# Scores of the global queries moved into the row-tiled run of the local scores, in two PSUM banks, and the last output tile in three pieces

## The chip, the cores and the metric

The kernel runs on one NeuronCore of a Trainium2 chip. The metric is the time on the device in microseconds (us). The profile of one execution covers a slightly shorter span (315.8 us where the time is 317.6), and all times inside an execution are counted from its start. Every run quoted here was fast: one core, granted TensorE clock 0.993 to 1.00.

TensorE does the matmuls and writes to PSUM, of which this kernel uses eight banks of 512 fp32 columns on 128 partitions. ScalarE (ACT) and VectorE (DVE) read the banks; POOL (GpSimd) casts inputs. The first matmul of a new tile waits until the last reader of the tile that had its bank before has ended; in the trace of the changed kernel it then starts some 53 ns later.

## The reference, cut to what matters

```python
# batch 8, heads 8, 512 local and 32 global positions, head size 64; window 32
s_g  = scale * q_g @ concat(k_g, k_l).T            # 32 global queries see all 544 keys
out_g = softmax(s_g) @ concat(v_g, v_l)
s_ll = where(|i - j| <= 32, scale * q_l @ k_l.T, -1e9)
s_lg = scale * q_l @ k_g.T                         # local queries see window and global keys
out_l = softmax(concat(s_lg, s_ll)) @ concat(v_g, v_l)
x = concat(out_g, out_l)  -> (4352, 512)           # tokens x (heads * head size)
h = x @ w_in                                        # 512 -> 2048
out = (h * clip(h + 3, 0, 6) / 6) @ w_out           # 2048 -> 512
```

## The kernel before: the parts that matter

The unit of the attention part is a pair of heads, `p` (32 pairs, 4 per batch `b`). The second matrix product pair (called MoE in the code) is cut into units that are dealt out between the steps of attention by `M(n)`: 16 units `u1` per batch (four matmuls of 512 columns into a bank psH, then a relu on ScalarE and a multiplication `gt` on VectorE that frees the bank), then 16 units `u2` (four matmuls into a bank po, copied out after four units). The loop over the last 24 pairs:

```python
psp = tile_pool(name="psp", bufs=7, space=PSUM)     # seven rotating banks
psg = tile_pool(name="psg", bufs=1, space=PSUM)     # one for the global output
...
    M(n[0])
    ...
    if p + 1 < NPAIR:
        emit_S2(p + 1)        # local scores: row-tiled, four banks psS
    M(n[1])
    if p + 1 < NPAIR:
        emit_SG(p + 1)        # global scores: full height, one bank psSG
    ...
    M(n[2])
    emit_AV(p)                # probabilities times values, two banks pav
    emit_PG(p)
    M(n[3])
```
```python
def emit_S2(p):
    pss = [ps_tile(f"psS{i}") for i in range(4)]
    for ch in range(2):
        for w in (*range(1, NT), 0):
            ...
            for e in range(2):                      # head e lies on 64 of the 128 rows
                r = slice(e * D, (e + 1) * D)
                nc.tensor.matmul(out=pss[2 * ch + e][:, w * P:(w + 1) * P],
                                 lhsT=kT[r, c0:c0 + P], rhs=qT[r, w * P:(w + 1) * P])
    ...                                             # four exponentials, four masks

def emit_SG(p):
    ps = ps_tile("psSG")
    qz = qgz[:, m, b].rearrange("p e s -> p (e s)") # 2 x 32 columns, half of them zeros by rows
    for u in range(NT + 1):                         # five matmuls, 128 rows, 64 columns
        c0 = u * KW if u < NT else D
        nc.tensor.matmul(out=ps[:, u * 2 * Sg:(u + 1) * 2 * Sg], lhsT=kT[:, c0:c0 + P], rhs=qz)
    nc.scalar.activation(out=Eg[:, 0:NT]..., in_=ps[:, 0:NT * 2 * Sg], func=EXP, ...)
    nc.scalar.activation(out=Eg[r, NT]..., in_=ps[r, NT * 2 * Sg:(NT + 1) * 2 * Sg], func=EXP, ...)
```

A row-tiled matmul here uses 64 of the array's 128 rows, and the two heads run side by side: in the trace their matmuls start in twos, 3 to 4 ns apart.

The softmax here doesn't subtract the row's maximum and nothing guards it: scores larger than these inputs give would overflow.

## Time and profile before

| | before |
|---|---|
| time, median | 317.6 us |
| TensorE busy | 96% |
| VectorE, ScalarE, POOL busy | 68%, 63%, 48% |
| pair period, in the stretch from 172 to 250 us | 8.34 to 8.45 us |

TensorE never waits in that stretch. "Busy" alone would not tell that: it needs the timeline, where the starts of successive TensorE rows leave no gap. The prediction shows the rows. Three lines belong beside them, the shapes of the two global-score exponentials and of the matmul, from the groups by shape (columns: operation, shapes, count | busy us, mean ns | idle before):

```profile
L358 ACT ACTIVATE Eg<-psSG 128x256 f16<-128x256 f32 x32 | 13.0, 406 | 1.2 <-PE psSG L357 1.1
L361 ACT ACTIVATE Eg<-psSG 32x64 f16<-32x64 f32 x32 | 6.9, 215 | 0.8
L357 PE MATMUL psSG<-qgz,kT 128*128 128x64 f16 x160 | 9.2, 193 | 0.8 <-DVE qgz L213 0.8
```

The mean of a matmul (193 ns) is its length from start to modelled end, not its share of the stream: the five follow one another every 29 ns.

### The profile page before, as it was taken

How to read it: one execution, taken by the hardware profiler on the slowest of the kernel's cores; microseconds unless marked ns; L12 is line 12 of the kernel's file. 1: busy time of each engine (PE TensorE's matmuls, PEld its weight loads, DVE VectorE, ACT ScalarE, POOL GpSimd, SP SyncE). 2: the span in 40 equal slices, each digit the busy share in tenths (PEclk: the TensorE clock that was granted, in tenths of full speed). 3: DMA queues.
4: the chain of work that ended last, by engine and by line, in shares of the span. 5: the costliest groups of instructions: out<-in, count | busy, mean ns of one | idle time of the engine just before them, and what ended most of it. 6: DMA issues, size and time to landing. Idle time of an engine off the chain costs nothing.

```text
span 315.8 us, 7343 instructions
## 1 busy us (share of the span) xinstructions
PE 304.3 (96%) x2688; PEld 161.9 (51%) x2688; DVE 213.9 (68%) x484; ACT 200.1 (63%) x417; POOL 152.6 (48%) x273
## 2 busy tenths in 40 slices
PE   6898899999999999999999999999999999999995
PEld 4554555545555555555555555555555544448444
DVE  5678688898765799569945996468943962479101
ACT  6657877887444985479844993589556941579000
POOL 3878987599866475764574558542511000000000
PEclk9999999999999999999999999999999999999999
DMA  7999999999999999999997999896642002100131
GB/s 207 243 295 333 302 300 317 213 185 211 217 201 238 180 183 191 180 229 193 181 154 152 215 187 205 177 232 106 114 103 86 17 19 83 66 2 1 37 98 66
DMA packets 140260, 53.05 MB, mean 168 GB/s; under 512 B 127552, under 2 KB 131904, under 8 KB 140224
## 3 DMA queue, kind: packets, MB, share of 16 engines
q1 hardware_dynamic: 138048, 52.32, 78.3%
q0 software_dynamic: 2176, 0.26, 2.0%
q8 instruction: 21, 0.34, 0.5%
q14 instruction: 15, 0.12, 0.2%
HBM read 35.13 MB, written 8.91 MB: 139 GB/s over the span
## 4 chain that ended last, share of the span: by engine, by line
PE 81%; DVE 8%; ACT 6%; issue 2%; DMA 2%; SPq 0%; POOL 0%
PE po L488 34%; PE psH L472 32%; PE psS L297 3%; DVE gt L479 3%; PE pav L383 2%; PE pav L386 2%; ACT t L477 2%; DVE xn L391 2%; DMA stg<-in_q_l_dram 2%; DVE E L304 2%; PE psSG L357 1%; PE psS L326 1%; ACT E L335 1%; PE po L500 1%; ACT E L301 1%
## 5 line engine op out<-in xcount | busy, mean ns | idle before, releaser
L488 PE MATMUL po<-wout,gt 128*128 128x512 f16 x528 | 122.6, 379 | 0.0
L472 PE MATMUL psH<-xt,win 128*128 128x512 f16 x512 | 119.6, 379 | 1.4 <-POOL win L174 1.0
L479 DVE SCALAR_TENSOR_TENSOR gt<-t,psH 128x512 f16<-128x512 f32 (+1 forms) x144 | 90.1, 652 | 20.9 <-ACT t L477 19.8
L477 ACT ACTIVATE t<-psH,half_col 128x512 f32<-128x512 f32 (+1 forms) x144 | 91.8, 670 | 18.0 <-PE psH L472 16.8
L472 PEld LDWEIGHTS <-win 128*128 128x128 f16 x576 | 53.1, 98 | 52.8 <-POOL win L174 1.8
L488 PEld LDWEIGHTS <-gt 128*128 128x128 f16 x528 | 48.4, 98 | 52.2
L304 DVE TENSOR_TENSOR E<-E,mk 128x512 f16<-128x512 f16 x96 | 51.3, 569 | 30.4 <-ACT E L301 29.0
L301 ACT ACTIVATE E<-psS 128x512 f16<-128x512 f32 x96 | 49.9, 605 | 13.5 <-PE psS L297 13.4
L492 ACT COPY ot<-po 128x512 f32<-128x512 f32 x16 | 9.4, 586 | 58.6 <-PE po L488 53.1
L140 POOL CAST kn<-stg 128x512 f16<-128x512 f32 x31 | 19.8, 640 | 34.7 <-DMA stg<-in_k_l_dram 33.1
L391 DVE TENSOR_TENSOR xn<-pav,rc 128x256 f16<-128x256 f32 x64 | 26.1, 422 | 1.3
L409 POOL TENSOR_TENSOR s<-Eg 128x128 f32<-128x128 f16 x24 | 10.4, 434 | 33.8 <-ACT Eg L358 32.6
L492 DVE COPY ot<-po 128x512 f32<-128x512 f32 x17 | 11.7, 690 | 21.2 <-PE po L488 21.1
L140 POOL CAST qn<-stg 128x512 f16<-128x512 f32 x31 | 20.3, 656 | 11.3 <-DMA stg<-in_q_l_dram 11.3
L140 POOL CAST vt<-stg 128x512 f16<-128x512 f32 x32 | 21.1, 658 | 9.7 <-DMA stg<-in_v_l_dram 9.4
L144 POOL COPY vb<-vt 64x512 f16<-64x512 f16 x32 | 20.2, 631 | 2.1
L383 PE MATMUL pav<-vt,E 128*128 128x65 f16 x256 | 20.1, 194 | 0.0
L386 PE MATMUL pav<-vb,E 128*128 128x65 f16 x256 | 19.9, 195 | 0.0
L335 ACT ACTIVATE E<-psS 128x512 f16<-128x512 f32 x32 | 16.9, 600 | 4.8 <-PE psS L326 4.8
L383 PEld LDWEIGHTS <-E 128*128 128x128 f16 x256 | 17.9, 99 | 3.4
L386 PEld LDWEIGHTS <-E 128*128 128x128 f16 x256 | 16.8, 97 | 3.2
L297 PEld LDWEIGHTS <-kT 64*128 64x128 f16 x384 | 10.9, 94 | 10.1 <-issue 8.1
(93 smaller groups left out, 274.1 us busy)
## 6 DMA issues: line engine op xcount, KB each, us to landing
stg<-in_k_l_dram SPq DMA_DIRECT2D x32, 256.0 KB, 3.5
stg<-in_q_l_dram SPq DMA_DIRECT2D x32, 256.0 KB, 4.1
stg<-in_v_l_dram SPq DMA_DIRECT2D x32, 256.0 KB, 4.9
out_dram<-ot SPq DMA_DIRECT2D x23, 256.0 KB, 3.6
stg<-in_moe_w_in_dram SPq DMA_DIRECT2D x16, 256.0 KB, 6.0
stg<-in_moe_w_out_dram SPq DMA_DIRECT2D x16, 256.0 KB, 5.1
out_dram<-ot SPq DMA_DIRECT2D x8, 192.0 KB, 3.9
out_dram<-ot SPq DMA_DIRECT2D x16, 64.0 KB, 2.4
```

Of the source, the lines that this page charges most:

```text
L140: eng.tensor_copy(out=o, in_=s[c + "f"])
L297: nc.tensor.matmul(out=pss[2 * ch + e][:, w * P:(w + 1) * P], lhsT=kT[r, c0:c0 + P], rhs=qT[r, w * P:(w + 1) * P])
L301: nc.scalar.activation(out=E[:, ch, e], in_=pss[2 * ch + e], func=EXP, scale=qk_scale)
L304: nc.vector.tensor_tensor(out=E[:, ch, e], in0=E[:, ch, e], in1=mk[:, ch].rearrange("p w c -> p (w c)"), op=mult)
L383: nc.tensor.matmul(out=o, lhsT=E[:, 0, e, w * P:(w + 1) * P], rhs=vt[:, w, m, c], start=True, stop=False, skip_group_check=True)
L386: nc.tensor.matmul(out=o, lhsT=E[:, 1, e, w * P:(w + 1) * P], rhs=vb[:, (w - 1) % NT, m, c], start=False, stop=True, skip_group_check=True)
L391: nc.vector.tensor_tensor(out=xn[:, 2 * w2:2 * w2 + 2].rearrange("p w (e d) -> p w e d", e=2), in0=po[:, :, 1:1 + P].rearrange("p w (e d) ...
L472: nc.tensor.matmul(out=ps[:, 0:n], lhsT=w_in_t[m][:, c * P:(c + 1) * P], rhs=rhs(m), start=(m == 0), stop=(m == NM - 1), skip_group_check= ...
L477: nc.scalar.activation(out=t1[:, 0:n], in_=ps[:, 0:n], func=RELU, bias=half_col, scale=1.0 / 6.0)
L479: nc.vector.scalar_tensor_tensor(out=gts[c][:, 0:n], in0=t1[:, 0:n], scalar=1.0, in1=ps[:, 0:n], op0=amin, op1=mult)
L488: nc.tensor.matmul(out=po[t][:, 0:dm], lhsT=gts[c][:, t * P:(t + 1) * P], rhs=w_out_t[c // 4][:, c % 4], start=(c == 0), stop=(c == NC - 1))
L492: (nc.scalar.copy if t % 2 else nc.vector.tensor_copy)(out=ot, in_=po[t][:, 0:dm])
```

## The change

The full-height matmul multiplies half zeros: 128 rows by two heads' columns, of which each head needs 64 rows. The change drops the zeros and computes each head apart, two at a time, inside the run that is row-tiled anyway, so that no further change of tiling is needed. The two heads' scores go to a bank each (the prediction names the page that asks for this). The exponentials keep their place but are now four, two for each head: they come after the next units, as before. Apart from that, the last output tile is cut into 256 + 128 + 128 columns instead of 256 + 256, to shorten the last copy and transfer.

```diff
 def emit_S2(p):
 ...
+        psG = [ps_tile(f"psSG{e}") for e in range(2)]
+        for u in range(NT + 1):
+            c0 = u * KW if u < NT else D
+            for e in range(2):
+                r = slice(e * D, (e + 1) * D)
+                nc.tensor.matmul(out=psG[e][:, u * Sg:(u + 1) * Sg], lhsT=kT[r, c0:c0 + P], rhs=qgz[r, m, b, e])
         for ch in range(2):
             ...                                   # exponentials and masks of the local scores
+        return psG
 ...
+    def exp_G(p, ps):
+        Eg = Egs[p % NE]
+        r = slice(D, D + Sg)
+        for e in range(2):
+            nc.scalar.activation(out=Eg[:, 0:NT, e],
+                                 in_=ps[e][:, 0:NT * Sg].rearrange("p (u s) -> p u s", u=NT),
+                                 func=EXP, scale=qk_scale)
+            nc.scalar.activation(out=Eg[r, NT, e], in_=ps[e][r, NT * Sg:(NT + 1) * Sg],
+                                 func=EXP, scale=qk_scale)
+        sum_E(p)
 ...
+        PARTS = [(0, dm // 2), (dm // 2, 3 * dm // 4), (3 * dm // 4, dm)]
 ...
-            emit_S2(p + 1)
+            psG = emit_S2(p + 1)
         M(n[1])
-            emit_SG(p + 1)
+            exp_G(p + 1, psG)
```

More of the change, by code (lines that the diff above doesn't have):

```diff
@@ L287, in emit_S2 @@
     def emit_S2(p):
+        b, m = divmod(p, NM)
         s = st[p]
@@ L351, in emit_SG @@
         kT = st[p]["kT"]
-        Eg = Egs[p % NE]
         ps = ps_tile("psSG")
@@ L362, in emit_SG @@
                              in_=ps[r, NT * 2 * Sg:(NT + 1) * 2 * Sg], func=EXP, scale=qk_scale)
-        if b >= NRUN:
-            sum_E(p)
+    def exp_G(p, ps):
+        Eg = Egs[p % NE]
+        r = slice(D, D + Sg)
[6 more added lines that the diff above has]
+        sum_E(p)
     xts = {}
@@ L494, in u2, with u2_part @@
                     nc.sync.dma_start(out=out[row:row + nr, :], in_=ot[r0:r0 + nr, :])
-        def u2_half(t, h):
-            hs = slice(h * dm // 2, (h + 1) * dm // 2)
+        PARTS = [(0, dm // 2), (dm // 2, 3 * dm // 4), (3 * dm // 4, dm)]
+        def u2_part(t, k):
+            hs = slice(*PARTS[k])
+            w = hs.stop - hs.start
             ps = ps_tile("po")
             for c in range(NC):
-                nc.tensor.matmul(out=ps[:, 0:dm // 2], lhsT=gts[c][:, t * P:(t + 1) * P],
+                nc.tensor.matmul(out=ps[:, 0:w], lhsT=gts[c][:, t * P:(t + 1) * P],
                                  rhs=w_out_t[c // 4][:, c % 4, hs], start=(c == 0), stop=(c == NC - 1))
             ot = wrk.tile([P, dm], FP32, tag="ot", name="ot", bufs=4)
-            (nc.vector.tensor_copy if h else nc.scalar.copy)(out=ot[:, 0:dm // 2], in_=ps[:, 0:dm // 2])
+            (nc.vector.tensor_copy if k != 1 else nc.scalar.copy)(out=ot[:, 0:w], in_=ps[:, 0:w])
             for r0, nr, row in dests[t]:
-                nc.sync.dma_start(out=out[row:row + nr, hs], in_=ot[r0:r0 + nr, 0:dm // 2])
+                nc.sync.dma_start(out=out[row:row + nr, hs], in_=ot[r0:r0 + nr, 0:w])
         if last:
@@ L509, in moe_units @@
                     + [lambda t=t, c4=c4: u2(t, c4) for t in range(n // P - 1) for c4 in range(NC // 4)]
-                    + [lambda h=h: u2_half(n // P - 1, h) for h in range(2)])
+                    + [lambda k=k: u2_part(n // P - 1, k) for k in range(len(PARTS))])
         first = [u1] if early else [lambda c=c: u1(c) for c in range(NC)]
@@ L815 @@
     pin(*ALL)
-    emit_S2(2 * NM)
+    psG = emit_S2(2 * NM)
     M(2)
-    emit_SG(2 * NM)
+    exp_G(2 * NM, psG)
     wrap_q(2 * NM + 1)
@@ L857 @@
     emit_XG(B - 1)
-    tail = units[-(NC - 2):]
-    del units[-(NC - 2):]
+    tail = units[-(NC - 1):]
+    del units[-(NC - 1):]
     units += moe_units(
```

## The prediction

> **What bounds the kernel now.** I read the page's busy shares and its chain of waits first, then the groups of instructions by shape, then the timeline of one pair of heads, engine by engine.
>
> ```profile
> span 315.8 us, 7343 instructions
> ...
> PE 304.3 (96%) x2688; PEld 161.9 (51%) x2688; DVE 213.9 (68%) x484; ACT 200.1 (63%) x417; POOL 152.6 (48%) x273
> ...
> PE 81%; DVE 8%; ACT 6%; issue 2%; DMA 2%; SPq 0%; POOL 0%
> ```
>
> TensorE is the bound: 304.3 of 315.8 us busy. A table of stretches puts its idle time at the two ends: between 156 and 260 us it has none, between 103 and 156 us a total of 0.55 us. So any wait that the change puts in front of TensorE between 70 and 250 us is paid in full, and any stream time that it removes is gained in full.
>
> The change works on "pairs" (two heads of a batch), the last 24 of 32. One of them, on TensorE:
>
> ```profile
> 180.18 0.59 PE L472 MATMUL psH<-xt,win 128*128 128x512 f16 x2
> 180.71 0.62 PE L297 MATMUL psS<-qT,kT 64*128 64x128 f16 x16
> 181.26 1.90 PE L472 MATMUL psH<-xt,win 128*128 128x512 f16 x8
> 183.00 0.31 PE L357 MATMUL psSG<-qgz,kT 128*128 128x64 f16 x5
> 183.14 1.89 PE L472 MATMUL psH<-xt,win 128*128 128x512 f16 x8
> ```
>
> First column start, second length (us); the differences of the starts are what counts, as lengths overlap. The local scores (L297, row-tiled: 64 rows, two heads side by side) take 181.26 - 180.71 = 0.55 us. The global scores (L357) take 183.14 - 183.00 = 0.14 us, one matmul per 29 ns. Nothing waits.
>
> Who empties the PSUM banks in that stretch:
>
> ```profile
> 180.81 0.69 ACT L477 ACTIVATE t<-psH,half_col 128x512 f32<-128x512 f32 x1 [0.17 <-PE psH L472]
> 181.40 2.05 ACT L301 ACTIVATE E<-psS 128x512 f16<-128x512 f32 x4
> 183.31 1.30 ACT L477 ACTIVATE t<-psH,half_col 128x512 f32<-128x512 f32 x2
> 184.45 0.43 ACT L358 ACTIVATE Eg<-psSG 128x256 f16<-128x256 f32 x1
> 184.91 0.22 ACT L361 ACTIVATE Eg<-psSG 32x64 f16<-32x64 f32 x1
> ```
> ```profile
> 180.28 1.95 DVE L479 SCALAR_TENSOR_TENSOR gt<-t,psH 128x512 f16<-128x512 f32 x3
> 182.14 2.31 DVE L304 TENSOR_TENSOR E<-E,mk 128x512 f16<-128x512 f16 x4
> ```
>
> With s = 180.71, the start of the local scores: the three psH banks filled before s come free when VectorE ends its three gt's, at s + 0.25, s + 0.85 and s + 1.51; the four psS banks when ScalarE ends its four exponentials, at s + 1.28, 1.77, 2.26 and 2.74. There are seven such banks (the eighth accumulates the global output). Now, four go to psS at s, and three more are asked for at s + 0.55, 1.43 and 2.29 (psH, psH, psSG). Each is free when it is asked for (0.25, 0.85 and 1.28). The schedule fits seven banks with little to spare.
>
> **What the Trainium skill says.** "TensorEngine Tiling (Array Packing)", Restrictions and Gotchas: row tiling raises PSUM pressure, as row tiles need different banks. That is why the change needs two banks for what took one. The same page, Instruction Overhead, gives a matmul some 60 cycles whatever its columns below that; the trace does better (below). Its Key Properties say that changing the tiling mode drains the array. The trace agrees: from the start of the last pair of row-tiled matmuls to the next full-height one is 148 ns, 53 of them its 128 columns (at the 2.4 columns per ns of L472's 214 ns for 512), so 95 ns are lost; a similar 94 ns precede the run. "ScalarE: Activation LUTs", What ACT_TABLE_LOAD costs, gives an ACTIVATE with immediate scale and bias 186 ns plus 0.833 ns per column: 399 for 256 columns, and L358's mean is 406.
>
> **The change part by part.**
>
> *Global scores on TensorE.* Removed: 24 x 5 matmuls of 64 columns, 24 x 0.145 = 3.5 us; that is all that this part could ever gain. Added: 24 x 10 matmuls of 64 rows and 32 columns, in five pairs, in the run of L297. Streaming alone would be 13 ns a pair, but the trace has such pairs: the first part of a window in line L326, at 11.10 us, where the next pair starts 39 ns after a 32-column pair (41 after 96 columns, 55 after 128). So weight loads or issue set some 39 ns. The run grows from 7 x 55 + 148 = 533 ns to 8 x 55 + 4 x 39 + (148 - 40) = 704; entry unchanged, no second mode change. That is +171 for -145: **+0.026 us a pair, +0.6 us in all**. The halved columns give nothing.
>
> *Banks.* Six are now asked for at the run's start: four at s, two at s + 0.44. In the pair shown, psG0 is served (0.25), psG1 waits for the second psH at 0.85 plus about 0.05 for the signal (at 109.99 us TensorE started 57 ns after such a release). The next unit then asks for a seventh bank at s + 0.72 while its only candidates are psH (1.51) and the first psS (1.28): it starts at 1.33 at best, **0.61 us late**. The waiting chain is relu of the last psH, then the first exponential, and nothing in it depends on TensorE's backlog, so it recurs. I made the same list for all 24 pairs:
> - 8 pairs (70, 141, 149, 181, 189, 214, 223, 248 us) with psH units before the run and a new bank after it: 0.6 each, 4.9.
> - 2 pairs (110, 118 us) in the stretch where VectorE is behind; banks come free at s + 1.3, 1.9, 2.5 and s + 0.6, 1.5, 2.2: 0.5 and 0.86, together 1.4.
> - 2 pairs (126, 156 us) where an output accumulation stays open and psG1 waits for s + 0.83 and 1.03: 0.44 and 0.56, together 1.0.
> - the 12 others, after output units, whose bank is copied out by s + 0.6 to 0.8: 0.03 each, twice some 0.13, together 0.5.
>
> Sum: **+7.8 us**.
>
> *ScalarE.* 2 exponentials become 4. From 0.43 + 0.22 = 0.65 us to two of 128 columns (0.32 each, 0.43 less 128 x 0.833 ns) and two of 32 columns (0.2 each): 1.04, so +0.39 a pair, +9.4 us busy. Beside TensorE in most pairs; between 180 and 190 us ScalarE is 92% busy, but the waits above lengthen those pairs by 0.6, which makes room. I charge 0.
>
> *Last tile.* 256 + 256 columns become 256 + 128 + 128. TensorE: 16 x 109 ns become 32 x 56 = +0.05 us. The last copy (L503, 0.42 us) shrinks by 128 columns, some 0.13 us, and its transfer, 1.7 us to land, halves in bytes, of which I expect little: 0.1. Together **-0.2 us**. Neutral.
>
> Sum: 317.6 + 0.6 + 7.8 - 0.2 = 325.8. I take 0.8 off, as the compiler may issue other ready matmuls (the accumulation of the global output, 0.15 us a pair) into a wait, and as some waits may overlap ones already there: **325.0 us**, +2.3%.
>
> **Rivals.**
> 1. *The stream wins.* Pairs of 32 columns run in their 13 ns, and the banks come free as needed: 5 x 13 = 65 ns, less the 40 saved at the run's end, replace 145, which saves 24 x 0.12 = 2.9 us: 314.5 us with the tail. For it: the intent, and that TensorE is the bound. Against: the 39 ns seen, and seven banks, all spoken for in the list above. It can't pass 2%.
> 2. *Waits are filled.* Banks are assigned so that the two long-held ones never meet the psH units, or the order shifts around the wait; then only the +0.6 remains, 318 us. For it: half of the pairs have spare banks anyway. Against: in 8 pairs no bank at all is free.
> 3. *ScalarE becomes the bound* in the stretches of psH units: psG0 and psG1 are held until the global exponentials come, after the relus of the next units (at s + 4 or later), so five banks serve the rest, and relus come 0.39 us later each pair. Up to 24 x 0.39 more, 330 us or above. For it: 92% busy there, so its idle time elsewhere (37% of the span) can't help. Against: those stretches are only half of the pairs.
>
> **Range and chances.** Rival 2 in part (half of the waits filled) gives 321; rival 3 in part 329. Range 319.5 to 329.5. Two per cent above is 324.0, just below my centre: slower by over 2% with 0.60, same 0.38, faster 0.02, for no part can gain 6 us.
>
> **What would show it.** TensorE's groups should show idle time in front of the global scores and of the first psH or po matmul after them, released by "ACT E L301" or "DVE gt", some 0.6 us in about half of the pairs, and TensorE's busy share some 2 points lower. The pitch of the new pairs should be near 39 ns; if it is 13, step one is wrong. ScalarE should be some 9 us busier. If the idle in front of TensorE is under 2 us in sum, the bank list is wrong: then banks were assigned or work ordered otherwise than I assumed. If waits for psH in mid-pair appear, rival 3 is at work.

## The result, and the profile after

The changed kernel takes 325.99 us (325.42 to 326.47, 4 runs) against 317.6 us (316.94 to 317.78, 4 runs). The ratio is 1.0267, with a 95% interval of 1.0244 to 1.029. Ratios here and below are the mean time of one kernel's fast runs over the mean of the other's fast runs of the same rounds, so they are not quite the ratio of the medians.

The same pair of heads on TensorE, after the change (line numbers have moved: local scores L298, global scores L305, psH units L489):

```profile
184.85 0.62 PE L298 MATMUL psS<-qT,kT 64*128 64x128 f16 x16
185.65 0.17 PE L305 MATMUL psSG<-qgz,kT 64*128 64x32 f16 x1 [0.18 <-DVE gt L496]
186.24 0.27 PE L305 MATMUL psSG<-qgz,kT 64*128 64x32 f16 x9 [0.42 <-DVE gt L496]
186.45 3.63 PE L489 MATMUL psH<-xt,win 128*128 128x512 f16 x16
```

From the start of the local scores to the next unit it is now 186.45 - 184.85 = 1.60 us; before, it was 0.55, with 0.14 later for the global scores. The brackets say what ended the idle time: the first global-score matmul waited for a gt of VectorE, that is, for a psH bank, and the second, of the other head, for the next one. The gaps between starts are larger than the bracketed idle, because TensorE counts as busy until the modelled end of its pipeline. By the clock of starts, the first waits from s + 0.46 to s + 0.80 and the second from there to s + 1.40 (s = 184.85).

ScalarE in the same stretch, and VectorE's gt's:

```profile
184.95 0.69 ACT L494 ACTIVATE t<-psH,half_col 128x512 f32<-128x512 f32 x1 [0.18 <-PE psH L489]
185.54 2.05 ACT L308 ACTIVATE E<-psS 128x512 f16<-128x512 f32 x4
187.52 0.69 ACT L494 ACTIVATE t<-psH,half_col 128x512 f32<-128x512 f32 x1
188.11 0.27 ACT L376 ACTIVATE Eg<-psSG 128x128 f16<-128x128 f32 x1
```
```profile
184.32 2.47 DVE L496 SCALAR_TENSOR_TENSOR gt<-t,psH 128x512 f16<-128x512 f32 x4
```

The relu of the last psH unit, then the four exponentials, as before; the global exponentials come from 188.11 on, 2.5 us after psSG was first written, and until then they hold two banks. The gt's that the two heads wait for end at s + 0.75 and s + 1.34; before the change the gt's of the same place ended at s + 0.25 and s + 0.85. That they come half a microsecond later is taken up under "Is it ScalarE?".

A second kind of pair, where output units follow and the global scores get banks sooner, and a third without any wait:

```profile
229.12 0.62 PE L298 MATMUL psS<-qT,kT 64*128 64x128 f16 x16
229.57 0.59 PE L305 MATMUL psSG<-qgz,kT 64*128 64x32 f16 x10
230.45 0.38 PE L505 MATMUL po<-wout,gt 128*128 128x512 f16 x1 [0.29 <-ACT E L308]
```
```profile
168.16 0.62 PE L298 MATMUL psS<-qT,kT 64*128 64x128 f16 x16
168.61 0.28 PE L305 MATMUL psSG<-qgz,kT 64*128 64x32 f16 x10
168.82 0.60 PE L505 MATMUL po<-wout,gt 128*128 128x512 f16 x2
```

In the first, the next unit waits for the first exponential (1.33 us in all); in the second, the whole run takes 0.66 us, against 0.55 + 0.14 before. So the new matmuls are not slower than the old ones where nothing waits: they are faster, by 0.03 us a pair of heads.

The groups by shape, after:

```profile
L376 ACT ACTIVATE Eg<-psSG 128x128 f16<-128x128 f32 x48 | 13.9, 290 | 0.6
L379 ACT ACTIVATE Eg<-psSG 32x32 f16<-32x32 f32 x48 | 9.0, 188 | 1.1
L305 PE MATMUL psSG<-qgz,kT 64*128 64x32 f16 x240 | 8.8, 174 | 4.3 <-DVE gt L496 3.7 <-DVE qgz L213 0.3
```

The last column of L305 is the new wait, 3.7 of 4.3 us for gt (in idle by the modelled ends, so less than by starts). ScalarE's busy time went from 200.1 to 208.2 us.

Where the time went, pair by pair. A period runs from the first local-score matmul of a pair to that of the next (for the last pair, to the end); the table sums the differences, after less before, over the 24 pairs. The pairs are named by the time of their local scores before.

| pairs | periods after less before, us | the prediction's list |
|---|---|---|
| 8 with psH units ahead and a new bank behind (70, 141, 149, 181, 189, 214, 223, 248 us) | 0.62, 0.62, 0.43, 0.91, 0.62, 0.91, 0.62, 0.65: 5.4 | 4.9 |
| 110 and 118 us, VectorE behind | 0.47, 0.97: 1.4 | 1.4 |
| 126 and 156 us, an output accumulation open | 0.41, 0.61: 1.0 | 1.0 |
| the 12 others | between -0.26 and 0.58: 0.4 | 0.5 |
| sum | 8.3 | 7.8 |

The last pair's 0.65 contains the shorter tail; without it, the same pair loses 0.89.

How far the table can be trusted: from 126 us on, the periods of the runs repeat to about 0.02 us where the code is the same. Before that they don't: with only the tail changed (the first experiment) the period at 118 us is 0.53 longer and that at 74 us 0.10 longer, and with only the exponentials split (another one below) the one at 74 us is 0.31 shorter. So the agreement at 110 and 118 us, and that of the 12 others, is partly luck. The 12 others are not twelve small waits as in the list: they hold -0.26 at 74 us, +0.14 at 88 us and +0.57 at 102 us, where the wait is in mid-pair (5 us after the local scores one of the two pav tiles waits for a gt), and the remaining nine are at plus or minus 0.03. The spans of the two profiled runs differ by 7.8 us and not by 8.3: the part before the first of these pairs, which varies from run to run, was 0.4 us shorter in the second.

### The profile page after: what moved, and what is told of

It reads as the page before. It is cut to its first block, busy times and chain, and to the rows that moved or that the text cites. A ratio compares the mean times of both kernels' runs of the same rounds, so it can differ in the third digit from the quotient of the medians.

```text
span 323.6 us, 7657 instructions
## 1 busy us (share of the span) xinstructions
PE 307.5 (95%) x2824; PEld 165.5 (51%) x2824; DVE 213.4 (66%) x485; ACT 208.2 (64%) x465; POOL 152.4 (47%) x273
## 4 chain that ended last, share of the span: by engine, by line
PE 67%; DVE 14%; ACT 10%; DMA 3%; issue 3%; POOL 2%; SPq 1%; POOLq 0%; DVEq 0%; ACTq 0%
PE po L505 35%; PE psH L489 20%; DVE gt L496 7%; ACT t L494 4%; DVE xn L408 3%; ACT E L308 2%; PE pav L400 2%; PE pav L403 2%; DMA stg<-in_q_l_dram 2%; DMA stg<-in_v_l_dram 1%; PE psS L334 1%; PE psS L298 1%; ACT E L343 1%; PE po L520 1%; PE pg L440 1%
## 5 line engine op out<-in xcount | busy, mean ns | idle before, releaser
L505 PE MATMUL po<-wout,gt 128*128 128x512 f16 x528 | 120.7, 379 | 1.0 <-ACT E L308 0.9
L489 PE MATMUL psH<-xt,win 128*128 128x512 f16 x512 | 118.4, 379 | 1.1 <-ACT E L308 0.4
L494 ACT ACTIVATE t<-psH,half_col 128x512 f32<-128x512 f32 (+1 forms) x144 | 92.8, 668 | 18.5 <-PE psH L489 17.1
L489 PEld LDWEIGHTS <-win 128*128 128x128 f16 x576 | 54.0, 98 | 54.2 <-POOL win L174 1.4
L505 PEld LDWEIGHTS <-gt 128*128 128x128 f16 x528 | 49.8, 98 | 55.5 <-issue 0.9
L311 DVE TENSOR_TENSOR E<-E,mk 128x512 f16<-128x512 f16 x96 | 49.2, 550 | 32.1 <-ACT E L308 30.9
L308 ACT ACTIVATE E<-psS 128x512 f16<-128x512 f32 x96 | 49.8, 604 | 12.6 <-PE psS L298 12.5
L140 POOL CAST qn<-stg 128x512 f16<-128x512 f32 x31 | 19.4, 627 | 11.6 <-DMA stg<-in_q_l_dram 10.2
L144 POOL COPY vb<-vt 64x512 f16<-64x512 f16 x32 | 20.9, 654 | 2.0
L298 PEld LDWEIGHTS <-kT 64*128 64x128 f16 x384 | 10.9, 94 | 9.9 <-issue 8.0
```

Of the source, the lines that this page charges most:

```text
L140: eng.tensor_copy(out=o, in_=s[c + "f"])
L144: eng.tensor_copy(out=vbs[b % NV][0:D, :, m, vc], in_=vts[b % NV][D:P, :, m, vc])
L308: nc.scalar.activation(out=E[:, ch, e], in_=pss[2 * ch + e], func=EXP, scale=qk_scale)
L311: nc.vector.tensor_tensor(out=E[:, ch, e], in0=E[:, ch, e], in1=mk[:, ch].rearrange("p w c -> p (w c)"), op=mult)
L489: nc.tensor.matmul(out=ps[:, 0:n], lhsT=w_in_t[m][:, c * P:(c + 1) * P], rhs=rhs(m), start=(m == 0), stop=(m == NM - 1), skip_group_check= ...
L494: nc.scalar.activation(out=t1[:, 0:n], in_=ps[:, 0:n], func=RELU, bias=half_col, scale=1.0 / 6.0)
```

## The experiments

Theory: the loss comes from two more PSUM banks being asked for early, at the start of the local scores, where the banks of the preceding psH units are not yet empty. Rivals: the row-tiled matmuls cost more themselves; the added work of ScalarE is what delays; the tail costs. The output of all twelve kernels was accepted against the reference, even that of the two that compute something else (said where they come). Each experiment's ratio is to the kernel before as run in the same round (medians 317.51 to 317.94 us).

### One part at a time

The last tile in three pieces alone (the edit is that part of the diff above):

> The kernel before with only the last output tile in three pieces. My theory (the two early banks cause the whole loss): a shorter last copy and transfer, about 0.2 us less than before, 317.4 us. Rival (the smaller pieces cost TensorE or issue time at the end): 0.3 us or more above before.

Measured: 317.32 us (6 runs), ratio 0.9979 (0.9961 to 0.9997). In the trace, from the first matmul of the last tile to the end: 7.19 us before, 6.95 with three pieces. The tail gains a quarter of a microsecond and costs nothing; the rest of the 0.6 us between the medians is within the spread of the runs.

The scores alone (the last tile back in two pieces):

> The changed kernel with the last tile back in two pieces. If the scores carry the whole loss: 326.2 us, a ratio of 1.027 to before. If the tail carries part of it, less than that by that part.

Measured: 325.73 us, ratio 1.0245 (1.0221 to 1.0269). Its interval overlaps that of the whole change (1.0244 to 1.029), and its periods sum to 8.4 us against 8.3. The scores carry the loss, all of it.

### Is it the row-tiled work, or asking early?

The ten row-tiled matmuls with their two banks are kept, but move back to where the full-height ones were:

```diff
 def exp_G(p, ps):
+    ps = [ps_tile(f"psSG{e}") for e in range(2)]
+    for u in range(NT + 1):
+        ...                       # the ten row-tiled matmuls, taken out of emit_S2
     Eg = Egs[p % NE]
```

> The row-tiled global scores with their two banks and four exponentials, but issued where the full-height ones stood, after the next units. Bank theory: two banks are asked for at about 2.3 us after the start of the local scores, when the first two psS banks are free (1.28 and 1.77), so next to no waits; what is paid instead is one more mode change, 95 ns in and 105 ns out with 4 x 25 ns between against 145 ns, 0.16 us in each of 24 pairs: 321.3 us. Rival (row-tiled matmuls or four exponentials cost by themselves): 326 us or more.

Measured: 322.26 us, ratio 1.0155 (1.0121 to 1.0189), some 4.9 us, between the two expectations and near the first. Its trace, around one pair:

```profile
185.85 0.62 PE L298 MATMUL psS<-qT,kT 64*128 64x128 f16 x16
186.49 1.89 PE L491 MATMUL psH<-xt,win 128*128 128x512 f16 x8
188.31 0.29 PE L374 MATMUL psSG<-qgz,kT 64*128 64x32 f16 x10
188.53 1.04 PE L491 MATMUL psH<-xt,win 128*128 128x512 f16 x4
```

No idle is shown before L374; the banks are free by then. Most pairs grow by 0.18 us; in all 24 that makes 4.3 us, and it is the second change of tiling: TensorE starts L374 311 ns after a 512-column matmul that needs 214, so 97 are lost; the five pairs of matmuls start after 39, 25, 25 and 25 ns, and the next full-height matmul 108 after the last pair: 97 + 114 + 108 = 319 ns, less the 145 of the full-height version. The rest is waits in pairs with psH units (here 0.08 us before the psH unit at 186.49, where before there was none). The individual starts also settle what a pair of 32-column matmuls costs: 39 ns for the first pair of a run, 25 ns for each after that.

The converse: full-height matmuls, one bank and two exponentials as before, but asked for early:

```diff
 def emit_S2(p):
 ...
+    psG = ps_tile("psSG")
+    for u in range(NT + 1):       # five matmuls of 128 rows and 64 columns, right after the local scores
+        ...
```

> Full-height global scores as before (five matmuls, one bank, two exponentials), but issued directly after the local scores, where the change puts them. Bank theory: five banks instead of six, so in the 8 pairs between psH units the next unit waits for the second psH bank (0.85 against 0.69) and not for the first exponential: some 0.2 us each, with the pairs that are behind 319.5 us. Rival (asking early is what costs, whatever the number of banks): 324 us or more.

Measured: 320.28 us, ratio 1.0073 (1.0053 to 1.0094), +2.3 us. Asking for one bank early costs about three tenths of the 7.8 us that the scores alone cost in the same round. The five pairs with psH units from 181 us on lose between 0.17 and 0.24 us each, as expected; of the other three on the list, those at 70 and 141 us lose nothing and the one at 149 us 0.45. 0.6 to 0.9 is lost at 74, 102 and 118 us, where the periods vary anyway; at 74 us it is TensorE's transposes that wait for VectorE's xn, which is no wait for a bank.

### Is it ScalarE?

The kernel before, with the two global exponentials split by head and nothing else:

```diff
-    activation(out=Eg[:, 0:NT]..., in_=ps[:, 0:NT * 2 * Sg])     # and one of 32 x 64
+    for e in range(2):                                            # each on one head's columns
+        activation(out=Eg[:, 0:NT, e], in_=psv[:, 0:NT, e])
+        activation(out=Eg[r, NT, e], in_=psv[r, NT, e])
```

> The kernel before with the two exponentials of the global scores split into four, one head each; ScalarE gets some 8 us more work as in the changed kernel, TensorE and banks are untouched. Bank theory: same time, 317.6 us within 0.5. Rival (ScalarE is the bound in the stretches of psH units): up to 24 x 0.39 us more, 321 us or above.

Measured: 319.07 us, ratio 1.0054 (1.002 to 1.0088), some 1.7 us, with ScalarE busy 207.4 us. This was neither the nothing that I had expected nor the rival's 4 us: ScalarE's work does cost something. The trace shows how: in the pairs at 181, 214 and 248 us the first psH unit after the local scores waits until s + 0.80 for a gt, that is, for a bank that comes free later, and each loses 0.23 to 0.24 us. So it was tried inside the changed kernel. Here one exponential of 256 columns reads the first head's bank for both heads, and the small one reads the second bank (another computation); sizes and number are then as before the change, and both banks are still held:

```diff
-        for e in range(2): ...                                    # four exponentials
+        activation(out=Eg[:, 0:NT], in_=ps[0][:, 0:NT * Sg]... .to_broadcast([P, NT, 2, Sg]))
+        activation(out=Eg[r, NT], in_=ps[1][r, NT * Sg:(NT + 1) * Sg]... .to_broadcast([Sg, 2, Sg]))
```

> The changed kernel with two exponentials of the global scores of the old sizes instead of four (the large one reads one bank for both heads, the small one the other; wrong results on purpose, order, banks and TensorE unchanged). If the banks are the main cause and ScalarE's 8 us more work a smaller one on top, as the 1.5 us of the split exponentials without the change suggest: 324.4 us, and the pairs that lost 0.9 us lose 0.6. If ScalarE is the main cause: 320 us or less. If it plays no part with the banks held: 326 us.

Measured: 324.4 us, ratio 1.0202 (1.018 to 1.0223). The pair of heads looked at above:

```profile
184.95 0.62 PE L298 MATMUL psS<-qT,kT 64*128 64x128 f16 x16
185.40 0.18 PE L305 MATMUL psSG<-qgz,kT 64*128 64x32 f16 x1
185.81 0.27 PE L305 MATMUL psSG<-qgz,kT 64*128 64x32 f16 x9 [0.23 <-DVE gt L494]
186.28 0.59 PE L487 MATMUL psH<-xt,win 128*128 128x512 f16 x2 [0.20 <-ACT E L308]
```

The first global score no longer waits, the second waits until s + 0.86, and the next unit for the first exponential until s + 1.33: the waits of the prediction's list (0.85 and 1.28, plus about 0.05 for the signal). The pairs at 181 and 214 us, which lost 0.91, lose 0.62. So in the changed kernel ScalarE's extra work makes the psH banks come free half a microsecond later in those pairs, and takes 1.0 us of the 8.3 by the periods (2 us by the two ratios). The two differ mostly at 74 us, where this run lost 0.8 us more than the changed kernel, again by waits of the transposes for xn. The other 6 to 7 us are there without the split.

### Is it the number of banks?

First, the kernel before with one rotating bank less (`bufs=6`), and nothing else:

> The kernel before with six rotating PSUM banks instead of seven, nothing else. Bank theory: even without the change one bank less costs microseconds, since the first psH after the local scores waits for the second psH bank (0.85 us after their start, asked for at 0.55) and later units for exponentials: 321 to 324 us. Rival (banks are not what it hangs on): 318 us.

Measured: 321.77 us, ratio 1.0147 (1.0106 to 1.0187), +4.7 us, inside the expectation. Without the change, too, a bank less costs microseconds: seven were just enough.

Then one bank more. The accumulator of the global output holds the eighth bank. In these versions each pair's part goes to a rotating bank and is copied to SBUF by ScalarE, and the sums of the denominators use a rotating bank too:

```diff
-psp = tile_pool(name="psp", bufs=7, space=PSUM)
-psg = tile_pool(name="psg", bufs=1, space=PSUM)
+psp = tile_pool(name="psp", bufs=8, space=PSUM)
 def emit_PG(p):
-    o = pg[:, 0, m].rearrange("p e s -> p (e s)")
+    o = ps_tile("psPG")[:, 0:2 * Sg]
     ...
+    nc.scalar.copy(out=pgs[b][:, m].rearrange("p e s -> p (e s)"), in_=o)
```

> The kernel before with eight rotating banks: the accumulator of the global output gives up its own bank, each pair's part goes to a rotating bank and is copied to SBUF by ScalarE (32 copies of 64 columns, some 0.2 us each). It serves as the base for the next run. Bank theory: the few waits at the three pairs that are behind (1.1 us together) mostly go: 316.8 us; the copies are beside other work.

Measured, without the change: 317.1 us, ratio 0.9986 (0.995 to 1.0021). The periods sum to 1.2 us less than before, at 74, 110, 118 and 149 us (the largest, 0.45 us, at 110 us; at 110 and 149 us TensorE had waited for a gt before, and here the trace shows it idle nowhere in the 24 pairs). The profiled run is the fastest of the four, 1.2 us under their median.

> The changed kernel with the same eight rotating banks. Bank theory: psG1 and the next unit are served one release earlier (0.25 and 0.85 us after the start of the local scores), so some 0.2 us stay in 8 pairs and the rest of the loss goes: 319 us, within 2 us of its base with eight banks. Rival (the loss sits in TensorE or ScalarE work): it stays 8 us above its base.

Measured, with the change: 322.18 us, ratio 1.0147 (1.0113 to 1.0181): the loss against the base falls from 8.4 to 5.1 us (6.2 by the periods of the two profiled runs), and not to 2 as expected. The two accumulations that were open lose nothing any more, nor do most pairs before output units (down to the 0.03 us that they gain); of the 6.2 us, 3.8 are in the eight pairs with psH units (0.75 us each at 181 and 214 us, shown below), 1.7 at 110 and 118 us and 1.0 at 74 and 102 us:

```profile
183.91 0.62 PE L297 MATMUL psS<-qT,kT 64*128 64x128 f16 x16
184.36 0.18 PE L304 MATMUL psSG<-qgz,kT 64*128 64x32 f16 x1
184.76 0.27 PE L304 MATMUL psSG<-qgz,kT 64*128 64x32 f16 x9 [0.23 <-DVE gt L498]
185.36 0.59 PE L491 MATMUL psH<-xt,win 128*128 128x512 f16 x2 [0.32 <-DVE gt L498]
```

Four psH banks, not three, were still full at the start of these local scores (free at s + 0.21, 0.81, 1.40 and 2.00), for ScalarE now has the copies as well as the split exponentials. Taking the split away again tells whether that is so:

> The same two exponentials with eight rotating banks (wrong results on purpose). If what eight banks left of the loss (about 5 us above their base) comes from ScalarE being later, so that four psH banks are still full at the start of the local scores: 319 us. If not: 322 us.

Measured: 320.86 us, ratio 1.0097 (1.0074 to 1.012):

```profile
183.34 0.62 PE L297 MATMUL psS<-qT,kT 64*128 64x128 f16 x16
183.80 0.28 PE L304 MATMUL psSG<-qgz,kT 64*128 64x32 f16 x10
184.26 0.59 PE L489 MATMUL psH<-xt,win 128*128 128x512 f16 x2 [0.18 <-DVE gt L496]
```

Now the global scores run without a wait, and the next unit waits until s + 0.92 for a psH bank that is free at s + 0.86: 0.2 us lost in each of the five such pairs from 181 us on, which is what the bank list gives for eight banks. By the periods, this version is 3.9 us above its base: 2.3 of them in the stretch from 102 to 156 us, where ScalarE and VectorE are behind, and 1.1 in the first two pairs. The trace names the waits there: at 74 us (0.8 us) the transposes wait for VectorE's xn, which is no wait for a bank; at 110 and 149 us the second head and the next unit wait for gt's, at 118 us the next unit for the bank of the transposed global keys. Why VectorE is later there than in the base I have not taken apart; the total missed the expected 319 us by almost 2. This run is of a later round, on another chip, than its base, so the two are best compared by their ratios to the kernel before (1.0097 and 0.9986).

### Versions meant to beat both kernels

Eight banks and the last tile in three pieces, with full-height global scores in their old place:

> A version meant to beat both: the kernel before with eight rotating banks and the last tile in three pieces, full-height global scores where they were. The sum of the two parts measured apart (0.14% and 0.21%): 316.5 us, a ratio of 0.9965. If the parts don't add or the eight banks gain nothing: 317.3 us.

Measured: 316.99 us (6 runs), ratio 0.9974 (0.9951 to 0.9996). It is faster than the kernel before by a quarter of a per cent, with an interval that just leaves out 1; whether the eight banks add to what the tail alone gives (0.9979) these runs can't tell.

> The version above with the row-tiled global scores in those 12 pairs alone in which the trace with eight banks shows no wait after them, and the full-height ones in the other 12. Each of the 12 gained 0.03 us there: 0.35 us less than the version above, 316.1 us, if the added exponentials cost nothing in the stretches of output units. If they do: above it.

Measured: 317.73 us, ratio 1.0005 (0.9972 to 1.0037). This one missed. Nine of the 12 pairs gained their 0.03 us, and two lost 0.3; but a single wait of 1.5 us ate several times the gain (the pair after it got back 0.3 us), in a pair whose own global scores were full-height:

```profile
106.58 0.19 PE L447 MATMUL psPG<-Eg,vgs 128*128 128x64 f16 x1
108.29 2.75 PE L497 MATMUL psH<-xt,win 128*128 128x512 f16 x12 [1.52 <-DVE gt L504]
```

There the psH unit waited for its bank until 108.24 us, while the bank of the global scores had been free since 106.83: in the compiled program this tile had been given the other bank. The choice of banks is fixed when the kernel is compiled, and the releases came in another order. In the version before this one, without the edit, the same unit started without a wait (at 106.87 us). So a change in one pair can place a wait in another.

## Why the prediction was right, point by point

- **What bounds it.** TensorE's idle-free stretch: right. The periods sum to 8.3 us where the time grew by 8.4, and in the pairs from 181 us on each one's loss is its wait less the 0.03 us that the stream gained.
- **The bank list.** Right in kind, and mostly in size (the table above). In the version with two exponentials, six of the eight pairs with psH units lose 0.62 us, and the last one too if the 0.25 of the tail is given back; the list had 0.6. The eighth, at 149 us, loses 0.4, because there the kernel before waits 0.25 us already, which the list overlooked. The sum for the 12 others is luck: nine lose or gain 0.03, and their 0.4 us come mostly from one wait in mid-pair at 102 us that was not on the list. The tile asked for starts 53 ns after its bank's last reader ends (185.593 to 185.647 us for the first head's bank, 186.190 to 186.243 for the second's), which the list took as about 0.05.
- **The stream of the global scores: the step that failed.** The prediction took 39 ns for a pair of 32-column matmuls and got +0.6 us. The runs show 25 ns, and 0.03 us gained per pair where nothing waits, at most 24 x 0.03 = 0.7 us in all (where the next unit waits for a bank anyway, a shorter run changes nothing). The 39 ns had been read at the only line where the kernel before has such matmuls, and there they are always the first of a run: after a change of tiling the first step is longer (39 ns for 32 columns at six of the eight places, and 66 against 55 for 128 in the local scores). I took an edge for a steady state. The same line held a warning: 41 ns for the 96 columns that follow are about what their streaming takes (96 / 2.4 = 40). So "the halved columns give nothing" was wrong, and the rival that the stream wins was right about the sign, though not about its 13 ns.
- **ScalarE, "I charge 0".** Mis-sized: 1.0 us by the periods, 2 us by the ratios. The busy time was right (+8.1 against +9.4 us); what was wrong is that the added waits would always make room. They do where a wait has just been: at 189 us, in the pair after the one that lost 0.91, the loss is 0.62, as listed. But in the pair at 172 us nothing waits, so nothing makes room for the longer exponentials; relus and gt's fall half a microsecond behind, and at 181 us 0.6 us of waiting becomes 0.9 (the same at 214 and 248 us).
- **The tail.** -0.25 us against -0.2.
- **The 0.8 us taken off** for the compiler filling waits. That happened in one pair, at 119 us, where the accumulation of the global output was issued between the two heads' scores; in the 23 others TensorE's order stayed. The deduction was too large.
- **The sum.** +0.6 became up to -0.7, ScalarE added 1 to 2, the list's waits came out near their size, and the deduction was not earned: 325.0 forecast, 325.99 measured. The errors of the parts partly cancelled: that the total is this close is luck, while the places and the kind of the waits are not.
- **TensorE's busy share** was to fall by some 2 points and fell by 1.4 (304.3 of 315.8 us to 307.5 of 323.6): part of the waiting is counted as busy, because a matmul's end is modelled. The starts show it, the share hides part of it. The sign of rival 3, a wait in mid-pair, appeared in one pair, at 102 us; since it is there with the old exponentials too (0.55 us), it isn't ScalarE's added work that makes it.

## What to carry to other kernels

Before moving an operation to an earlier place, list the buffers that it takes there: for each, when the last reader of the tile that held it finishes, against when it is now asked for. That list, made from one trace, gave this result to within a microsecond (with some luck in the sum, as said above), whereas the arithmetic saved (3.5 us at the very most, 0.7 at most in fact) said nothing about it. And when a cost is read from a trace, check that it was not read at the edge of a run.

## What the Trainium skill lacked or had wrong

- "TensorEngine Tiling (Array Packing)", Instruction Overhead: some 60 cycles per matmul, with one column as slow as 60. Row-tiled pairs of 64 x 32 matmuls start every 25 ns, both heads together, so 12.5 ns per matmul on average; 60 cycles are 25 ns at the 2.4 columns per ns seen here, so as a distance between starts the figure fits the pair, not the matmul.
- The same page, Key Properties, says that changing the tiling mode drains the array, without a size. Here: some 97 ns lost on the way in (311 ns less 214), 95 on the way out (148 less 53), and a first step some 11 to 14 ns longer; one more change of mode and back cost 0.18 us per pair of heads, with the faster matmuls already counted in.
- "ScalarE: Activation LUTs", What ACT_TABLE_LOAD costs: 186 ns + 0.833 ns per column is given for 128 partitions, and holds there for 128 columns (293 against a mean of 290 ns). It says nothing of fewer partitions: on 32 of them it is 25 ns too high (213 against 188 ns for 32 columns), on 64 it is 23 too high (293 against a mean of 270 ns for the logarithms of 128 columns).
- "PSUM — Partial Sum Buffer", the summary for kernel authors, asks to evacuate promptly, with no figure for the time from the end of a bank's last reader to the next matmul into it. Here it was 53 ns, and 50 to 57 ns at the other waits looked at.
- No page says that a compiled, fixed choice of banks can leave TensorE waiting on a full bank beside a free one: 1.5 us in one place of the last experiment.
